# Delta-rule attention and two MoE layers: four-way state update, a longer look-ahead, and another engine pair for the masking of the query products

## The chip, the core and the metric

The kernel runs on one core of a Trainium2 chip. The core's engines are TensorE (PE in the profile; PEld is its weight load), VectorE (DVE), ScalarE (ACT), GpSimd (POOL) and SyncE (SP, which issues the transfers). The metric is the device time of one execution in microseconds.

## The reference

Attention by the delta rule over 4 batches, 8 heads, 768 positions, head size 48, with a state matrix for each batch and head; then two feed-forward layers over 3072 tokens.

```python
for t in range(S):
    y[:, :, t] = einsum('bhd,bhde->bhe', q[:, :, t], state)
    v_old = einsum('bhde,bhd->bhe', state, k_n[:, :, t])
    state = state + beta_t * einsum('bhd,bhe->bhde', k_n[:, :, t], v[:, :, t] - v_old)
x = y as (3072, 384)
h = x @ w1_in; x = (h * tanh(softplus(h))) @ w1_out      # 384 -> 2048 -> 384
h = x @ w2_in; out = (h * clip(h + 3, 0, 6) / 6) @ w2_out
```

Here `k_n` is `k` divided by its norm.

## The kernel before, in words

**Chunks.** The sequence is cut into 24 chunks `t` of 32 positions; the four batches lie side by side in the 128 partitions, 32 each, and heads in pairs `j`, halves `r`. For a chunk the keys and queries are transposed (`T_pe`, L419, copied to `kqt` by ScalarE, L425), and multiplied with the keys (`G_pe`, L439, two PSUM banks `gps`, one for each `r`). The key part times beta and a lower mask becomes `an` (`G_ew`, L457); the query part times an upper mask becomes `mt` (`G_ew2`, L463, VectorE). Two chunks of `an` go through DRAM to the layout of a forward substitution on VectorE (`substs`, tiles `ash`, `tp`, `tmp`, L716 and L723), which inverts them; the result comes back as `pt`, scaled by beta on GpSimd (`scale`, L744).

**Recurrence** (`rec`, L825). For each chunk, in this order: K (`state_pe`, `ksps`, keys times state), `r` (L862, the values less that), U (`U_pe`, `ups`, `pt` times `r`), the query round (`state_pe`, `yps`, queries times state), `u` copied to SBUF, MU (`MU_pe`, `mt` times `u` on top of the query round), the update round (`S_mm`, L808, `dsps`, keys times `u`), and eight VectorE additions to the state `sbd` (`S_add`, L820). The output is transposed (`X_pe`) and copied to `xst` (L972), four chunks to a block of 512 tokens.

The update round has two halves of two batches each, one PSUM bank a half; within a half the two batches alternate:

```python
for b in (2 * half, 2 * half + 1):
    p = slice(C * b, C * (b + 1))
    nc.tensor.matmul(out=S_part(b, r)[:, j, :], lhsT=kp(t)[p, j, r, 0:D], rhs=ut[t][p, 2 * j + r, :], ...)
```

`S_part(b, r)` lies in bank `b // 2`, partitions from `64 * (b % 2)`. A float32 matmul call shows in the trace as two matmul records and two weight loads.

**Look-ahead.** Inside chunk `t` (from 4 or 5 on) the recurrence also issues the transposes of chunk `t + 4`, after U, and the Gram products of chunk `t + 3`, after K. Keys have five buffers in rotation (`kp`), `kqt` and `mt` four; a key load waits for the update round that last read its buffer. The norms of the keys (`norms`: a square, a sum, a power on GpSimd, L399, and small VectorE steps, L401 to L367) and the beta mask (`beta_mask`, L407) must be done before the Gram products are issued. Chunks 0 to 7 are prepared by other functions (`prep_k`, `matrices`, `preps`, `preps_m`).

**MoE.** The first layer runs in six blocks of 512 tokens, 16 units each: nine `hps` matmuls (`mm1`, L1120), Mish on ScalarE (L1151), a split of the result into two parts (`ghi` on ScalarE, L1126, and `glo` on GpSimd, L1160), nine `o` matmuls (`mm2_t`, L1141). A block's input is split from `xst` into `xh` (ScalarE, L1098) and `xl` (VectorE, L1102). Weights are split in the same way by a lane of ScalarE and VectorE steps (`Weights`). The second layer follows, without the attention.

**Order.** `Flow` writes the program: each piece of work is a generator that names the events it needs, the engine and an estimated time, and the piece that can begin first (plus its penalty) is emitted next. Each engine then runs its queue strictly in that order. In the stage of the attention, five PSUM banks are shared by recurrence, look-ahead and `hps`; `room` grants a bank and `release` gives it back.

Of the kernel before, what the change touches and what calls it, by code (L numbers as in the profile page):

```python
# [16 lines left out]
C = 32  # L17
NKP = 5
NQP = 2
NVT = 3  # L20
NKQ = 4

RATE, TOKENS = 32.0, 110.0
# [103 lines left out]
def tile_delta_rule__moe_mish__moe_hardswish(  # L127
# [38 lines left out]
    with tc.manual_schedule():  # L166
# [84 lines left out]
        def load_heads(src, dst, t, engs=None):  # L251
# [5 lines left out]
            return flow.landed(2.2)  # L257

        def kp(t):
            return kpad[t % NKP]  # L260

# [33 lines left out]
        def loads_k():  # L295
            for t in range(NKP, NS):
                yield f"S{t - NKP}"
                yield LOAD
                flow.ev[f"kk{t}"] = load_heads(k, kp(t).rearrange("p j r d -> p (j r) d")[:, :, 0:D], t)
                if t >= 8:  # L300
                    flow.ev[f"k{t}"] = flow.ev[f"kk{t}"]
# [120 lines left out]
        def T_ew(t, i):  # L422
            if i == 0:
                kqt[t] = ap_.tile([128, NP, B, 2, C], F32, tag=f"kqt{t % NKQ}", name="kqt")
            nc.scalar.activation(  # L425
# [34 lines left out]
        def G_ew2(t, r):  # L460
            if r == 0:
                mt[t] = ap_.tile([128, H, C], F32, tag=f"mt{t % 4}", name="mt")
            nc.vector.tensor_tensor(  # L463
# [115 lines left out]
        def masks():  # L579
            for t in range(8, NS):  # L580
                yield f"n{t}"
                yield f"mt{t - 1}" if t > 8 else "G7"
                yield "POOL", 0.7
                beta_mask(t)
                flow.set(f"mb{t}")

        def G_post(t):

            for r in range(2):
                yield "DVE", 0.28  # L590
                G_ew(t, r)
            for r in range(2):
                yield "DVE", 0.28
                G_ew2(t, r)
                release(("G", t, r))
            flow.set(f"mt{t}")
            if t % 2:
# [3 lines left out]
                nc.sync.dma_start(out=an[g].rearrange("p s j -> s p j"), in_=x.rearrange("s t h j -> s (t h) j"))  # L601
                flow.ev[f"ad{g}"] = flow.landed(1.5)

        def T_post(t, i):
# [194 lines left out]

        def S_mm(t, half):  # L800

            if t == 0 or t >= 4:
                dps[half] = bank(("S", half), [128, 2, NP, D], "dsps")
            for r in range(2):
                for j in range(NP):
                    for b in (2 * half, 2 * half + 1):
                        p = slice(C * b, C * (b + 1))
# [4 lines left out]
                        )  # L812
            if half:
                flow.set(f"S{t}")

# [9 lines left out]
        def rec():  # L825


            for t in range(NS):
# [79 lines left out]
                if t < 4:  # L908
                    if t == 0:
                        yield room(("S", 0), ("S", 1))  # L910
                    yield "PE", 1.1, None, 64
                    for half in range(2):
                        S_mm(t, half)
                    flow.add(mu(t), pen=0.02)
# [4 lines left out]
                if not last:  # L919
                    yield room(("S", 0), ("S", 1))  # L920
                yield "PE", 1.0 if last else 2.6, None, 128
                MU_pe(t)
                flow.add(take_y(t), pen=0.05)
                if not last:
                    for half in range(2):
                        S_mm(t, half)
                    for b in range(B):
# [530 lines left out]
        flow.add(norms(), pen=0.05)  # L1458
        flow.add(preps(), pen=busy(0.1, 0.05), margin=busy(0.0, 1.0))
        flow.add(preps_m(), pen=busy(0.3, 0.05), margin=busy(0.0, 1.0))  # L1460
        flow.add(masks())
# [44 lines left out]
```

## Time and profile before

| | |
|---|---|
| median of 3 runs | 1072.04 us (1067.91 to 1072.45) |
| profiled execution | 1072.36 us |
| its span, first to last instruction | 1070.5 us |
| granted TensorE clock, mean | 0.988 |
| TensorE busy | 1039.6 us (97%) |
| VectorE, ScalarE, GpSimd busy | 647.8, 444.9, 213.1 us |

Busy TensorE time is modelled from starts, so a busy TensorE may still be waiting inside a matmul. The chain of the profile is followed back from the last instruction; it is on TensorE for 87% of the span.

### The profile page before, as it was taken

The numbers are of one execution on the slowest core, as the hardware profiler recorded it, in microseconds if no ns is written. First come the engines' busy times: TensorE is split into PE (matmuls) and PEld (weight loads), VectorE is DVE, ScalarE is ACT, GpSimd is POOL, SyncE is SP. The second block draws the span as 40 slices with busy tenths as digits, with TensorE's granted clock in tenths as the row PEclk, the third lists the DMA queues.
The fourth block names the chain that finished last, engine by engine and source line by source line (L and its number), as shares of the span: only waits on it lengthen the run. The fifth ranks groups of instructions, "written<-read, shape, count | busy, mean of one in ns | idle before, by whom it ended". The sixth has DMA issues, their size and how long they took to land.

```text
span 1070.5 us, 30628 instructions
## 1 busy us (share of the span) xinstructions
PE 1039.6 (97%) x13242; PEld 866.3 (81%) x13242; DVE 647.8 (61%) x1492; ACT 444.9 (42%) x884; POOL 213.1 (20%) x224
## 2 busy tenths in 40 slices
PE   8899998999999999999999999999999999999997
PEld 5566876777888788878887887999999999999996
DVE  6667977969496757849671799944333343333432
ACT  4346445433453344344432656534333343333432
POOL 3303333233333333332322332000000000000000
PEclk9899999989999999999999999999999999999999
DMA  5644244241423332241310543402001020010101
GB/s 94 148 125 100 68 123 112 61 86 32 83 41 80 58 67 67 46 77 31 70 21 15 185 134 120 140 1 60 1 14 46 1 59 1 14 46 1 30 1 30
DMA packets 149063, 66.64 MB, mean 62 GB/s; under 512 B 133024, under 2 KB 136096, under 8 KB 148928
## 3 DMA queue, kind: packets, MB, share of 16 engines
q1 hardware_dynamic: 146432, 63.84, 24.7%
q8 instruction: 104, 1.70, 0.6%
q10 hardware_dynamic: 2496, 0.84, 0.4%
q14 instruction: 31, 0.25, 0.1%
HBM read 51.02 MB, written 13.63 MB: 60 GB/s over the span
## 4 chain that ended last, share of the span: by engine, by line
PE 87%; DVE 7%; issue 2%; ACT 1%; POOL 1%; DMA 1%; POOLq 0%; ACTq 0%; DVEq 0%; SPq 0%
PE hps L1120 35%; PE p L1278 19%; PE o L1141 14%; PE warm L1437 3%; PE dsps L808 3%; PE tps L419 2%; PE gps L439 2%; PE yps L778 2%; PE ksps L758 2%; PE ups L768 2%; PE qps L665 2%; PE yps L758 1%; DVE cw L1065 1%; DVE cw L1062 1%; PE xps L956 1%
## 5 line engine op out<-in xcount | busy, mean ns | idle before, releaser
L1120 PE MATMUL hps<-xh,wih 128*128 128x512 f32 x576 | 229.3, 398 | 6.7 <-DVE mt L463 3.6
L1120 PE MATMUL hps<-xl,wih 128*128 128x512 f32 x576 | 227.3, 395 | 3.3 <-DVE xl L1102 3.3
L1120 PE MATMUL hps<-xh,wil 128*128 128x512 f32 x576 | 227.3, 395 | 0.0
L1160 POOL TENSOR_TENSOR glo<-g,ghi 128x512 fp32r<-128x512 f32 x96 | 130.4, 1358 | 307.4 <-ACT ghi L1126 244.7
L1253 DVE SCALAR_TENSOR_TENSOR r<-r,hps 128x512 f32<-128x512 f32 x96 | 66.1, 688 | 162.4 <-ACT r L1251 162.4
L1251 ACT ACTIVATE r<-hps,half_c 128x512 f32<-128x512 f32 x96 | 66.1, 689 | 171.3 <-PE hps L1120 171.2
L1151 ACT ACTIVATE g<-hps 128x512 f32<-128x512 f32 x96 | 57.1, 595 | 183.9 <-PE hps L1120 179.0
L1120 PEld LDWEIGHTS hps<-xh,wih 128*128 128x128 f32 x576 | 108.5, 188 | 29.3 <-issue 4.5
L1278 PE MATMUL p<-woh,glo 128*128 128x384 f32 x384 | 129.6, 337 | 0.0
L1278 PE MATMUL p<-woh,ghi 128*128 128x384 f32 x384 | 129.4, 337 | 0.0
L1278 PE MATMUL p<-wol,ghi 128*128 128x384 f32 x384 | 129.0, 336 | 0.0
L1120 PEld LDWEIGHTS hps<-xl,wih 128*128 128x128 f32 x576 | 108.5, 188 | 23.8 <-DVE xl L1102 4.7
L1120 PEld LDWEIGHTS hps<-xh,wil 128*128 128x128 f32 x576 | 108.6, 188 | 23.0
L716 DVE TENSOR_TENSOR tmp<-tp,ash 128x126 f32<-128x126 f32 (+22 forms) x248 | 99.1, 400 | 39.0 <-DMA ash<-ad 32.6
L1141 PE MATMUL o<-ghi,woh 128*128 128x512 f32 x288 | 114.2, 396 | 0.0
L1141 PE MATMUL o<-ghi,wol 128*128 128x512 f32 x288 | 113.9, 395 | 0.0
L1259 DVE TENSOR_TENSOR glo<-r,ghi 128x512 fp32r<-128x512 f32 x96 | 66.5, 693 | 57.0 <-ACT ghi L1126 56.5
L1126 ACT ACTIVATE ghi<-r 128x512 fp32r<-128x512 f32 x96 | 60.6, 631 | 64.6 <-DVE r L1253 64.5
L1141 PE MATMUL o<-glo,woh 128*128 128x512 f32 x288 | 84.2, 394 | 0.0
L723 DVE TENSOR_TENSOR tp<-tp,tmp 128x126 f32<-128x126 f32 (+22 forms) x248 | 79.5, 321 | 7.1
L820 DVE TENSOR_TENSOR sbd<-sbd,dsps 48x192 f32<-48x192 f32 x152 | 53.5, 352 | 43.6 <-PE dsps L808 40.6
L1278 PEld LDWEIGHTS p<-woh,ghi 128*128 128x128 f32 x384 | 72.3, 188 | 3.9
(139 smaller groups left out, 1436.3 us busy)
## 6 DMA issues: line engine op xcount, KB each, us to landing
raw<-in_moe_w_in_dram SPq DMA_DIRECT2D x24, 512.0 KB, 3.7
raw<-in_moe_w_out_dram SPq DMA_DIRECT2D x32, 384.0 KB, 3.1
vt<-in_v_dram SPq DMA_DIRECT2D x96, 48.0 KB, 2.2
x2d<-x2out SPq DMA_DIRECT2D x6, 768.0 KB, 4.0
x2in<-x2d SPq DMA_DIRECT2D x6, 768.0 KB, 6.2
kpad<-in_k_dram SPq DMA_DIRECT2D x88, 48.0 KB, 2.3
qpad<-in_q_dram SPq DMA_DIRECT2D x88, 48.0 KB, 2.1
out_dram<-osb SPq DMA_DIRECT2D x22, 192.0 KB, 3.1
```

What stands on the lines that cost most here:

```text
L716: nc.vector.tensor_tensor(out=tv, in0=x[:, 0:m, j:j + 1].to_broadcast([128, m, n]), in1=a[:, j + 1:C, j:j + 1].rearrange("p i o -> p o i") ...
L723: nc.vector.tensor_tensor(out=x[:, 0:m, j + 1:C], in0=x[:, 0:m, j + 1:C], in1=tv, op=ALU.add)
L820: nc.vector.tensor_tensor(out=o, in0=o, in1=S_part(b, r), op=ALU.add)
L1120: nc.tensor.matmul(out=ps[0], lhsT=w[:, kk, c], rhs=xhl[n][xi][:, kk, :], start=(kk == 0 and x == 0), stop=(kk == KD - 1 and x == 2))
L1126: nc.scalar.activation(out=hi, in_=g, func=ACTF.Copy)
L1141: nc.tensor.matmul(out=acc[i][dc], lhsT=w[:, e, 128 * dc:128 * (dc + 1)], rhs=a, start=(f == 0 and x == 0), stop=(f == KF - 1 and x == 2))
L1151: nc.scalar.activation(out=g, in_=ps, func=ACTF.Mish)
L1160: nc.gpsimd.tensor_tensor(out=lo, in0=g, in1=hi.bitcast(F32), op=ALU.subtract)
L1251: nc.scalar.activation(out=r, in_=ps, func=ACTF.Relu, scale=1.0 / 6.0, bias=half_c)
L1253: nc.vector.scalar_tensor_tensor(out=r, in0=r, scalar=1.0, in1=ps, op0=ALU.min, op1=ALU.mult)
L1259: nc.vector.tensor_tensor(out=lo, in0=r, in1=hi.bitcast(F32), op=ALU.subtract)
L1278: nc.tensor.matmul(out=acc[n][s], lhsT=a[:, c], rhs=w[:, e, :], start=(f == 0 and x == 0), stop=(f == KF - 1 and x == 2))
```

## The change

The update round takes all four batches in turn, in one group instead of two halves. From chunk 9 on, transposes are issued five chunks ahead, and from chunk 10 on, Gram products four chunks ahead; chunk 13 is prepared by a generator of its own (`extra`), in buffers that the weight conversion of the first layer has given up, so that keys have six buffers from there on, and `kqt` and `mt` five. For chunks 8 to 23 the query products are copied out of PSUM by ScalarE and masked by GpSimd in SBUF; the banks of the Gram products are released after these copies and the multiplies by beta. The next beta mask waits for the multiply by beta, no longer for `mt`.

```diff
+TX = 13
+        def slot(t, n):
+            while t > TX:
+                t -= n + 1
+            return "x" if t == TX else t % n
         def kp(t):
-            return kpad[t % NKP]
+            i = slot(t, NKP)
+            return more["k"] if i == "x" else kpad[i]
         def loads_k():
             for t in range(NKP, NS):
-                yield f"S{t - NKP}"
+                yield "more" if t == TX else f"S{t - NKP - (t > TX)}"
...
         def masks():
-                yield f"mt{t - 1}" if t > 8 else "G7"
+                yield f"an{t - 1}.1" if t > 8 else "G7"
...
         def G_post(t):
+            flow.add(M_post(t), pen=0.05)
             for r in range(2):
                 yield "DVE", 0.28
                 G_ew(t, r)
-            for r in range(2):
-                yield "DVE", 0.28
-                G_ew2(t, r)
-                release(("G", t, r))
-            flow.set(f"mt{t}")
+                flow.set(f"an{t}.{r}")
...
+        def extra():
+            yield "lo1.27"
+            more["k"], more["m"] = [x2p.tile([128, 512], F32, tag="x2", name=f"x{n}") for n in "km"]
...
+            nc.gpsimd.memset(more["k"][:, :, :, D:64], 0.0)
+            flow.set("more")
+            yield f"k{TX}"
+            yield f"q{TX}"
+            yield f"Tq{TX - 1}"
...
+            for i in range(2):
+                T_pe(TX, i)
+                flow.add(T_post(TX, i), pen=0.05)
+            flow.set(f"Tq{TX}")
+            yield f"kq{TX}"
+            yield f"mb{TX}"
...
+            G_pe(TX)
+            yield from G_post(TX)
+
+        def M_post(t):
+            m = slot(t, 4)
+            m = mt[t] = more["m"] if m == "x" else ap_.tile([128, H, C], F32, tag=f"mt{m}", name="mt")
+            for r in range(2):
+                yield "ACT", 0.3
+                G_raw(t, 1, r, m)
+                yield f"an{t}.{r}"
+                release(("G", t, r))
+            yield "POOL", 0.66
+            nc.gpsimd.tensor_tensor(out=m, in0=m, in1=masku.rearrange("p (o c) -> p o c", o=1).to_broadcast([128, H, C]),
+                                    op=ALU.mult)
+            flow.set(f"mt{t}")
...
-        def S_mm(t, half):
+        def S_mm(t):
             if t == 0 or t >= 4:
-                dps[half] = bank(("S", half), [128, 2, NP, D], "dsps")
+                for half in range(2):
+                    dps[half] = bank(("S", half), [128, 2, NP, D], "dsps")
             for r in range(2):
                 for j in range(NP):
-                    for b in (2 * half, 2 * half + 1):
+                    for b in range(B):
...
-                tk = t + 4 if 4 <= t < NS - 4 else None
+                tk = t + 4 if 4 <= t < TX - 4 else t + 5 if TX - 4 <= t < NS - 5 else None
-                tg = t + 3 if 5 <= t < NS - 3 else None
+                tg = t + 3 if 5 <= t < TX - 3 else t + 4 if TX - 3 <= t < NS - 4 else None
...
-                yield "PE", 1.0 if last else 2.6, None, 128
+                yield "PE", 1.0 if last else 2.0, None, 128
```

## Rows read from the trace of the kernel before

**Rows 1.** Busy time by stretch: start:end, length, then each engine's busy us.
```profile
100.00:214.00 114.00, 108.17 (x2309) 86.01 (x2307) 96.44 (x231) 55.83 (x125) 35.69 (x30) 0.99 0.35 89
214.00:661.00 447.00, 441.27 (x6356) 357.22 (x6356) 312.52 (x823) 192.16 (x411) 150.87 (x141) 0.99 0.31 70
```
**Rows 2.** Waits of TensorE: waiter, releaser: us in total, times, longest.
```profile
PE hps L1120 <- DVE mt L463: 3.6, 5, 1.2
...
PE hps L1120 <- DVE xl L1102: 3.3, 2, 2.6
PE hps L1120 <- DVE bnat L367: 2.6, 1, 2.6
```
**Rows 3.** Timeline of TensorE in chunk 11: start, us, line, tiles, records.
```profile
292.66 0.86 PE L439 MATMUL gps<-kqt 48*32 48x64 f32 x64
...
297.07 0.88 PE L768 MATMUL ups<-r,pt 32*32 32x48 f32 x64
297.89 0.87 PE L758 MATMUL yps<-sbd,kqt 128*32 128x96 f32 x32
...
300.41 0.88 PE L778 MATMUL yps<-u,mt 32*32 32x48 f32 x64
301.22 1.51 PE L808 MATMUL dsps<-u,kpad 32*48 32x48 f32 x64
```
**Rows 4.** The update round's line: records, ns min/median/max, first and last start.
```profile
L808 PE MATMUL dsps<-u,kpad x1472: 202/203/312, 47.7 to 571.7; 32*48 32x48 f32 x184
```
**Rows 5.** The chain of waits in chunk 2: start us, us, what.
```profile
78.51 0.84 PE dsps L808 x30
79.35 0.73 issue
...
81.01 1.19 PE warm L1437 x5
```
**Rows 6.** Timeline of ScalarE where blocks 1 and 2 begin.
```profile
212.63 0.49 ACT L972 ACTIVATE xst<-xps 128x384 f32<-128x384 f32 x1 [4.33 <-PE xps L956]
213.15 0.63 ACT L1098 ACTIVATE xh<-xst 128x512 fp32r<-128x512 f32 x1
...
308.34 0.49 ACT L972 ACTIVATE xst<-xps 128x384 f32<-128x384 f32 x1 [1.99 <-PE xps L956]
...
311.73 0.63 ACT L1098 ACTIVATE xh<-xst 128x512 fp32r<-128x512 f32 x1 [2.49 <-PE hps L1120]
```
**Rows 7.** Timelines of four engines, from chunk 13's Gram products to chunk 12's U.
```profile
275.05 0.86 PE L439 MATMUL gps<-kqt 48*32 48x64 f32 x64
...
291.83 0.43 DVE L716 TENSOR_TENSOR tmp<-tp,ash 128x31 f32<-128x31 f32 x1 [2.22 <-DMA ash<-ad]
...
309.21 0.56 DVE L862 TENSOR_TENSOR r<-vt,ksps 128x384 f32<-128x384 f32 x1
...
328.21 0.19 DVE L723 TENSOR_TENSOR tp<-tp,tmp 128x16 f32<-128x16 f32 x1
...
338.57 1.26 POOL L744 TENSOR_TENSOR pt<-pt,bnat 128x256 f32<-128x256 f32 x2
...
340.53 0.88 PE L768 MATMUL ups<-r,pt 32*32 32x48 f32 x64
```
**Rows 8.** Lines of the masking: records, ns min/median/max, first and last start.
```profile
L463 DVE TENSOR_TENSOR mt<-gps,masku x40: 242/284/295, 97.2 to 507.6; 128x128 f32<-128x128 f32 x40
...
L468 ACT ACTIVATE mt<-gps x8: 272/275/277, 20.2 to 35.0; 128x128 f32<-128x128 f32 x8
...
L478 POOL TENSOR_TENSOR mt<-mt,masku x4: 725/734/776, 20.7 to 35.4; 128x256 f32<-128x256 f32 x4
```
**Rows 9.** Timeline of all engines around 360 us.
```profile
358.26 1.28 POOL L1160 TENSOR_TENSOR glo<-g,ghi 128x512 fp32r<-128x512 f32 x1
358.33 1.24 DVE L401 TENSOR_SCALAR nn<-nn 128x8 f32<-128x8 f32 x1 [0.70 <-POOL nn L399]
...
361.10 0.47 PE L1120 MATMUL hps<-xh,wih 128*128 128x512 f32 x1 [0.92 <-DVE mt L463]
```

More of the change, by code (lines that the diff above doesn't have):

```diff
@@ L257, in load_heads @@
             return flow.landed(2.2)
+        more = {}
+        def slot(t, n):
+            while t > TX:
+                t -= n + 1
+            return "x" if t == TX else t % n
         def kp(t):
-            return kpad[t % NKP]
+            i = slot(t, NKP)
+            return more["k"] if i == "x" else kpad[i]
         def kp_first(t):
@@ L423, in T_ew @@
             if i == 0:
-                kqt[t] = ap_.tile([128, NP, B, 2, C], F32, tag=f"kqt{t % NKQ}", name="kqt")
+                n = slot(t, NKQ)
+                kqt[t] = (cvp.tile([128, NP, B, 2, C], F32, tag="r1", name="kqt") if n == "x" else
+                          ap_.tile([128, NP, B, 2, C], F32, tag=f"kqt{n}", name="kqt"))
             nc.scalar.activation(
@@ L461, in G_ew2 @@
             if r == 0:
-                mt[t] = ap_.tile([128, H, C], F32, tag=f"mt{t % 4}", name="mt")
+                n = slot(t, 4)
+                mt[t] = more["m"] if n == "x" else ap_.tile([128, H, C], F32, tag=f"mt{n}", name="mt")
             nc.vector.tensor_tensor(
@@ L602, in G_post @@
                 flow.ev[f"ad{g}"] = flow.landed(1.5)
+        def extra():
+            yield "lo1.27"
+            more["k"], more["m"] = [x2p.tile([128, 512], F32, tag="x2", name=f"x{n}") for n in "km"]
+            more["k"] = more["k"].rearrange("p (j r d) -> p j r d", j=NP, r=2)
+            more["m"] = more["m"][:, 0:H * C].rearrange("p (h c) -> p h c", h=H)
+            yield "POOL", 0.4
+            nc.gpsimd.memset(more["k"][:, :, :, D:64], 0.0)
[3 more added lines that the diff above has]
+            yield f"Tq{TX - 1}"
+            yield room(("T", TX, 0), ("T", TX, 1))
+            yield "PE", 0.8, None, 32
+            for i in range(2):
[4 more added lines that the diff above has]
+            yield f"mb{TX}"
+            yield room(("G", TX, 0), ("G", TX, 1))
+            yield "PE", 0.8, None, 64
+            G_pe(TX)
[12 more added lines that the diff above has]
+            flow.set(f"mt{t}")
         def T_post(t, i):
@@ L812, in S_mm @@
                         )
-            if half:
-                flow.set(f"S{t}")
+            flow.set(f"S{t}")
         def S_add(t, b):
@@ L910, in rec @@
                         yield room(("S", 0), ("S", 1))
-                    yield "PE", 1.1, None, 64
-                    for half in range(2):
-                        S_mm(t, half)
+                    yield "PE", 0.8, None, 64
+                    S_mm(t)
                     flow.add(mu(t), pen=0.02)
@@ L924, in rec @@
                 if not last:
-                    for half in range(2):
-                        S_mm(t, half)
+                    S_mm(t)
                     for b in range(B):
@@ L1459, in tile_delta_rule__moe_mish__moe_hardswish @@
         flow.add(preps(), pen=busy(0.1, 0.05), margin=busy(0.0, 1.0))
+        flow.add(extra(), pen=0.05)
         flow.add(preps_m(), pen=busy(0.3, 0.05), margin=busy(0.0, 1.0))
```

## The prediction

> **What bounds the kernel now.** I read the busy time by stretch first, to see which engine fills each stage. From 100 to 661 us, where the attention chunks run between the units of the first MoE layer, TensorE is busy in all but 12 us of 561 [rows 1]; VectorE, the next, is busy in 409 of them. So a TensorE microsecond taken out of this stage is worth up to a microsecond, as long as nothing else comes to set the pace. Second, the waits of TensorE: the largest inside this stage are of `hps` matmuls that found their PSUM bank still held by the masking of the query products (`mt`, 3.6 us in five waits, and one of 2.6 us put down to `bnat`, which stands beside `mt` on the same queue), and of the first `hps` of a block on its input `xl` (3.3 us in two) [rows 2]. Third, the timeline of TensorE in one chunk, for the price of each group of small matmuls: U, the query round, MU, the update round (`dsps`) and the Gram products G [rows 3]. The update round is the odd one: 1.51 us for 64 matmul records, where U and MU take 0.88 us for as many of the same 48 columns. It runs in 23 chunks (1472 records, 64 each) [rows 4].
>
> Fourth, whether the recurrence keeps up, because a block of MoE cannot start before its four chunks are written. In the timeline of ScalarE the last copy into `xst` begins at 212.63 and the split for block 1 at 213.15; for block 2 it is 308.34 and 311.73 [rows 6]. The reader is to see that the recurrence is only 0.5 to 3.4 us ahead: it is a second bound, just behind TensorE. What holds it is the inverse. Chunk 12 had its `r` at 309.21, and its U only at 340.53, because its `pt` was scaled at 338.57; that comes from a substitution that began at 291.83 and ended at 328.21, on a Gram matrix multiplied at 275.05 in chunk 10 [rows 7].
>
> **The change part by part.** *Update round.* Before, a half round alternates two row strips of the array (batches 0 and 1, then 2 and 3); after, all four are alternated. What decides is how many matmuls overlap. Two strips give 1.51 us for 64, 23.6 ns each. U and MU alternate four 32-row strips and take 0.88 us, 13.8 ns each [rows 3]. The query round, also four tiles but 96 columns, takes 0.87 us for 32, 27.2 ns each, twice U: with four tiles the time goes by the columns streamed [rows 3]. The new order has four row strips but only two column strips (batches 0 and 2 share one, in different banks). G tells whether that hurts: its two row halves share column strips, in different banks, with 64 columns. Four at a time would need 13.8 x 64/48 = 18.4 ns each, 1.18 us; it takes 0.86 us [rows 3]. So tiles on one column strip do overlap there. Bounds: nothing gained (1.51 stays) and U's 0.88. I take 0.88, the nearest in columns and strips: 0.63 us a round.
>
> The Trainium skill (TensorEngine Tiling, Restrictions and Gotchas, Gotcha 1) speaks against this: different row tiles write to different banks and cannot access one bank at the same time. The update uses two banks for four row tiles, so by that rule two would still run at a time and the round would stay at 1.51 us, the sum losing its largest term. U's four row tiles write the one bank of `ups`, at different partitions, at 13.8 ns, so the trace does not agree with the rule read that strictly; it is rival A below.
>
> How many rounds count: 19 of the 23 lie in the saturated stage (chunks 4 to 22), 19 x 0.63 = 12.0 us. For chunks 0 to 3 TensorE is filling time with `warm` matmuls right after the update [rows 5], so I take nothing of their 4 x 0.63 = 2.5 us and keep it as a bound. For chunks 4 to 7 I also take nothing: block 1 started 0.5 us after its last chunk was written [rows 6], and the look-ahead is not changed for them, so what TensorE saves there may be spent waiting for that chunk. That leaves 15 x 0.63 = 9.5 us.
>
> Cost of the denser order: MU and the update together become 128 matmuls in 1.76 us instead of 2.39. Among groups of small matmuls the chain of waits shows stretches of issue inside a group, one of 0.73 us [rows 5]. Between two such bursts here stand whole MoE units, so I take nothing; the bound is 0.73 in each of 15 chunks, 11 us.
>
> *Masking of the query products.* For chunks 8 to 23, two VectorE multiplies of 0.284 us go (16 x 0.57 = 9.1 us), and come back as two ScalarE copies of 0.275 us and one GpSimd multiply of 0.734 us [rows 8]: 8.8 us on ScalarE and 11.7 us on GpSimd. Neither is full: together ScalarE is busy 248 us and GpSimd 187 us of the 561 [rows 1]. These cover the cost; were GpSimd not free, each would delay the `glo` split behind it by 0.73 us. The gain is the bank: it now comes free after the two multiplies by beta and a ScalarE copy, no longer after two more instructions at the back of VectorE's queue. The wait at 360 us shows it: GpSimd's `glo` ran from 358.26, VectorE's tiny `nn` step took 1.24 us beside it, everything behind was late, and `hps` stood 0.92 us for `mt` [rows 9]. Bounds: none of the 3.6 us, and all of it plus the 2.6 [rows 2]. VectorE's queue can still hold the beta multiply up, so I take 2.5 us.
>
> The Trainium skill (SBUF — State Buffer, Who interferes with whom) says that a VectorE instruction with two SBUF inputs, or in a two-port mode, and a GpSimd instruction that reads SBUF shut each other out for a whole instruction. The `nn` step beside `glo` agrees. By that rule the 16 new multiplies could cost VectorE up to the 11.7 us they last; it would not move the sum, as VectorE is not what sets the end, but it is what rival C lives on.
>
> *Look-ahead.* Transposes and Gram products are the same instructions in another place; one chunk (13) gets them on its own, in buffers that weight conversion has left, and one small memset is added. On TensorE this costs nothing. K loads for later chunks are issued one chunk sooner relative to use, on SP, with the same count. The beta mask and the norm must be ready one chunk sooner, which is a new place to wait on VectorE and GpSimd. What it brings: the product for chunk 12's inverse moves up by about a chunk. The substitution needed 291.83 to 328.21, and U followed `pt` by 2 us [rows 7], so the recurrence of chunks 12 to 23 may come forward by up to one chunk, a quarter of the 95.7 us between the last `xst` copies of two blocks [rows 6], 24 us. It has no term of its own: it is what lets the 9.5 us through, because without it the lead of 0.5 to 3.4 us would be used up after two or three blocks of 2.5 us each.
>
> Sum: 9.5 + 2.5 = 12.0 us. The profiled execution took 1072.36 us (span 1070.5 and 1.9 around it), 0.03% from the median, so I make it 1060.4, and say 1060.
>
> **The rivals.** *A, the update round stays as it is* (banks or column strips), or its gain goes into issue stalls. For it: only two banks; stalls of this kind exist [rows 5]. Against: U and G [rows 3]. Only the bank waits are left: 1072.4 - 2.5 = 1070.
>
> *B, the recurrence sets the pace.* TensorE saves 2.5 us a block but waits for `xst`. For it: leads of 0.5 and 3.4 us [rows 6]. Against: the inverse moves up. With the lead used once (3.4) and the bank waits (2.5): 1072.4 - 5.9 = 1066.5.
>
> *C, slower.* Place: GpSimd's queue. The new multiply waits there for ScalarE's copy, and `glo`, the norm's power and the beta mask wait behind it; the norm holds VectorE's queue, that the Gram bank, and that the next `hps`. Price: 2.6 us, the one wait of this kind before [rows 2]. To end over 1077.7 it must eat the 12 us and 5.3 more, 17.3/2.6, so seven such waits in 16 chunks. Time: 1078 to 1082. Before there was one.
>
> **How the numbers follow.** The forecast case has 0.75, A 0.10, B 0.10, C 0.05. Its own range: down to 12.0 + 2.5 + 3.6 + 2.6 + 3.3 = 24 us saved (all rounds, all waits of [rows 2]), 1048, which needs everything at once; up to 9.5 us saved less a few stalls, 1066. The range for 8 in 10 is 1051 to 1067.5: it takes in B, and leaves A, C and the far low end. A measurement of this kernel can tell about 0.5% (5.4 us) from no change, so faster means under 1066.7: the forecast case and half of B, 0.80. Same: A, the other half of B, 0.15. Slower: 0.05.
>
> **What would show it.** The update round: 0.88 us for 64 records in the timeline, and its busy time between 100 and 661 falling by 12 us; 1.5 us is A, 1.5 us with pieces and issue between is the feed. Bank waits: the lines of `hps` waiting for `mt` go or turn to ScalarE's copy. Look-ahead: the lead of `xst` over the split grows past 3.4 us in blocks 3 to 5; if TensorE instead waits for `xl` at block starts, it is B. C shows as `hps` waits behind `nn` and `glo`. The prediction is wrong if the stage from 100 us to the second layer shortens by less than 6 us, or by more than 20.

## The result, and the profile after

The changed kernel takes 1078.32 us (median of 6 runs, 1074.92 to 1080.76), the kernel before 1069.97 (6 runs beside it, 1066.94 to 1072.45). The ratio is 1.0071, 95% interval 1.0053 to 1.009: 7 to 8 us slower, where 1060 was forecast and the range ended at 1067.5. The profiled execution took 1077.8 us, span 1076.1.

Three of the steps can be seen to do what they were costed to do. First the timeline of TensorE, an update round and the matmul behind it, and the update round's line (busy us, mean ns, then idle time ahead of it):

```profile
290.57 0.93 PE L857 MATMUL dsps<-u,kpad 32*48 32x48 f32 x64
291.43 0.50 PE L1166 MATMUL hps<-xh,wih 128*128 128x512 f32 x1
...
L857 PE MATMUL dsps<-u,kpad 32*48 32x48 f32 x1344 | 21.0, 206 | 4.8 <-issue 4.8
```

Its 64 records span 0.93 us, where they spanned 1.51 [rows 3]; from its start to the next matmul a round takes 0.86 us, where it took 1.44. So 0.58 us a round are gained. Second, the waits of TensorE:

```profile
PE ksps L806 <- DVE sbd L868: 10.1, 16, 2.3
PE dsps L857 <- issue: 4.8, 5, 1.2
PE hps L1166 <- DVE xl L1148: 4.6, 8, 2.2
```

The waits of `hps` for `mt` and `bnat` [rows 2] are gone. In their place stands one that was not there: K waits 10.1 us, in 16 pieces, for VectorE's additions to the state (before, K waited 1.0 us in all, none of it for them). Third, the masking's lines, as costed from [rows 8], and the recurrence's later lead: chunk 12's U, the last `xst` copy of block 4's input, and the split that waits for it (timelines):

```profile
L481 ACT ACTIVATE mt<-gps 128x128 f32<-128x128 f32 x34 | 8.6, 274 | 13.5 <-DVE an L469 8.8 <-PE gps L451 4.7
...
L648 POOL TENSOR_TENSOR mt<-mt,masku 128x256 f32<-128x256 f32 x13 | 10.1, 779 | 24.2 <-ACT mt L481 24.1
```
```profile
327.52 0.88 PE L816 MATMUL ups<-r,pt 32*32 32x48 f32 x64
...
490.70 0.49 ACT L1018 ACTIVATE xst<-xps 128x384 f32<-128x384 f32 x1 [0.79 <-PE xps L1002]
...
513.76 0.63 ACT L1144 ACTIVATE xh<-xst 128x512 fp32r<-128x512 f32 x1 [2.76 <-PE hps L1166]
```

Chunk 12's U came at 327.52 in place of 340.53 [rows 7], and block 4's input was ready 23 us ahead of its use.

But the stage as a whole lost. From TensorE's timelines, the us from the first `hps` of a block to that of the next (for block 5, to the first `p` matmul, the output product of the second layer):

| | block 0 | 1 | 2 | 3 | 4 | 5 |
|---|---|---|---|---|---|---|
| before | 114.3 | 101.4 | 96.1 | 96.8 | 85.4 | 74.9 |
| after | 111.1 | 104.6 | 97.0 | 106.7 | 81.2 | 75.2 |

Block 1 lost what block 0 had gained, and block 3 lost most. Of its 9.9 us some four are work that moved: it now holds five update rounds in place of four, and block 4 two in place of three. The rest is new: TensorE is idle in block 3 for 5.6 us (1.2 before) and at 1.2 GHz for 10.2 us (none before).

Block 1 first. The same ScalarE rows for block 2, and the busy time by stretch:

```profile
312.71 0.49 ACT L1018 ACTIVATE xst<-xps 128x384 f32<-128x384 f32 x1 [5.03 <-PE xps L1002]
313.23 0.63 ACT L1144 ACTIVATE xh<-xst 128x512 fp32r<-128x512 f32 x1
```
```profile
100.00:214.00 114.00, 108.63 (x2254) 85.60 (x2253) 94.14 (x226) 59.69 (x137) 38.96 (x35) 0.97 0.37 92
214.00:661.00 447.00, 433.34 (x6317) 345.29 (x6316) 330.10 (x808) 199.01 (x437) 156.93 (x152) 0.98 0.33 74
```

Block 2's input came 4.4 us later than before, and its split followed at once (0.5 us; 3.4 in [rows 6]). TensorE's busy time between 214 and 661 us fell by 7.9 us, and VectorE's rose by 17.6 [rows 1]. The chain that ended last was 87% TensorE before; now it leaves TensorE. The page's shares, then the shares of the chain from 225 to 316 us (most of block 1 of the changed kernel) and from 411 to 518 us (its block 3):

```profile
PE 54%; DVE 19%; DMA 2%; issue 2%; POOL 1%; SPq 1%; ACT 1%; DVEq 0%; POOLq 0%; ACTq 0%
```
```profile
by line: DVE tmp L764 26.1%; DVE tp L771 20.6%; DVE sbd L868 12.0%; DMA ash<-ad 9.7%; issue 5.5%; POOL nn L409 3.7%; PE ksps L806 2.6%; SPq L254 1.9%; PE o L1187 1.7%; SPq L751 1.6%; DVE an L469 1.5%; PE hps L1166 1.5%; PE xps L1002 1.4%; S
by line: DVE tmp L764 27.7%; DVE tp L771 24.6%; DVE sbd L868 12.9%; issue 5.1%; DMA ash<-ad 4.4%; POOL nn L409 3.1%; PE hps L1166 3.0%; DMA td<-tp 2.7%; DVE xl L1148 2.7%; SPq L776 1.7%; PE o L1187 1.5%; PE ksps L806 1.4%; DVE nn L411 1.3%;
```

In the kernel before, the window from 225 to 316 us of the chain read:

```profile
by line: PE hps L1120 35.2%; PE o L1141 32.0%; PE dsps L808 6.3%; PE yps L778 3.6%; PE ksps L758 3.5%; PE gps L439 3.5%; PE tps L419 3.4%; PE ups L768 2.7%; PE yps L758 2.6%; PE xps L956 2.1%; DVE nn L401 1.4%; POOL nn L399 0.8%; ACT ghi L1
```

Now the substitution (`tmp`, `tp`) and the state additions carry it. Here is the end of block 1: TensorE's timeline, then VectorE's.

```profile
303.51 0.84 PE L857 MATMUL dsps<-u,kpad 32*48 32x48 f32 x55
305.59 0.31 PE L857 MATMUL dsps<-u,kpad 32*48 32x48 f32 x9 [1.25 <-issue]
308.19 0.50 PE L806 MATMUL ksps<-sbd,kqt 128*32 128x96 f32 x2 [2.29 <-DVE sbd L868]
...
310.36 1.49 PE L806 MATMUL ksps<-sbd,kqt 128*32 128x96 f32 x26 [0.23 <-DVE sbd L868]
311.77 0.90 PE L1002 MATMUL xps<-ident,y 128*128 128x128 f32 x3
312.60 1.19 PE L451 MATMUL gps<-kqt 48*32 48x64 f32 x64
...
316.40 0.80 PE L1166 MATMUL hps<-xl,wih 128*128 128x512 f32 x1
```
```profile
307.14 0.28 DVE L764 TENSOR_TENSOR tmp<-tp,ash 128x70 f32<-128x70 f32 x1
307.33 2.97 DVE L868 TENSOR_TENSOR sbd<-sbd,dsps 48x192 f32<-48x192 f32 x8
```

No matmul of the MoE is left between 300.1 and 313.9 us. TensorE ends the update at 305.9; VectorE, busy with the substitution, begins the additions at 307.33, and they take 2.97 us; K follows piece by piece. From 308.1 to 318.3 the granted clock is 1.2 GHz: the Gram products take 1.19 us in place of 0.86 [rows 3], and an `hps` record 0.63 to 0.80 us where one at 2.4 GHz takes 0.39. Such stretches in the stage add up to 27.3 us, against 10.2 before.

The waits of K come in three such groups of about 3 us, in blocks 0, 1 and 3. The one in block 3 is of another kind: VectorE's and TensorE's timelines together.

```profile
463.86 0.93 PE L857 MATMUL dsps<-u,kpad 32*48 32x48 f32 x64
464.72 0.50 PE L1166 MATMUL hps<-xh,wih 128*128 128x512 f32 x1
...
468.30 0.84 PE L1187 MATMUL o<-glo,woh 128*128 128x512 f32 x3
470.04 0.38 DVE L764 TENSOR_TENSOR tmp<-tp,ash 128x128 f32<-128x128 f32 x1
470.33 2.96 DVE L868 TENSOR_TENSOR sbd<-sbd,dsps 48x192 f32<-48x192 f32 x8
471.18 0.33 PE L806 MATMUL ksps<-sbd,kqt 128*32 128x96 f32 x2 [2.04 <-DVE sbd L868]
...
473.35 1.49 PE L806 MATMUL ksps<-sbd,kqt 128*32 128x96 f32 x26 [0.23 <-DVE sbd L868]
```

Eighteen MoE matmuls stand between the update and K here, and the recurrence is far ahead: this is chunk 19, which completes block 4's input, and that input was then ready 23 us early. Still TensorE waits, because VectorE begins the additions 5.5 us after the update, behind steps of the substitution; and the granted clock is 1.2 GHz for 6.8 us from 471.9. At the head of block 3, too, the input was 7.1 us early, and `hps` waited 2.15 us for `xl`, which stood on VectorE behind the norm (VectorE had waited 5.9 us for GpSimd's power step, and GpSimd 5.8 us for a transfer) and behind a step that GpSimd's `glo` had slowed (last section).

All of the loss lies in the stage. From the first `hps` to the first `p` it took 568.9 us before and 575.8 after. I split it over TensorE's timeline, each group of matmuls running to the start of the next, so that a wait counts to the group it follows:

| us | before | after | |
|---|---|---|---|
| update rounds | 27.3 | 24.4 | 19 x 0.86 = 16.3, and 8.1 of waiting |
| transposes ahead | 19.7 | 13.7 | the bank waits of `hps` had stood behind them |
| query rounds and MU | 33.4 | 32.3 | |
| K | 15.9 | 26.1 | waits for additions, and the clock |
| `hps` | 215.2 | 220.0 | waits for `xl`, and the clock |
| all else | 257.4 | 259.3 | |

The bare rounds gave 11.0 us and the bank waits about 6. Query rounds and MU gave 1.1 more. Some 25 us of new waits and slower matmuls took it all back: 8.1 behind the update, 10.2 in K, 4.8 in `hps`, 1.9 elsewhere. 25.0 less 18.1 is the 6.9 us by which the stage grew.

### The profile page after: what moved, and what is told of

Read it like the earlier page. It is cut to its first block, busy times and chain, and to the rows that moved or that the text cites. A ratio compares the mean times of both kernels' runs of the same rounds, so it can differ in the third digit from the quotient of the medians.

```text
span 1076.1 us, 30630 instructions
## 1 busy us (share of the span) xinstructions
PE 1037.3 (96%) x13252; PEld 856.9 (80%) x13252; DVE 656.9 (61%) x1460; ACT 453.7 (42%) x916; POOL 223.6 (21%) x241
## 4 chain that ended last, share of the span: by engine, by line
PE 54%; DVE 19%; DMA 2%; issue 2%; POOL 1%; SPq 1%; ACT 1%; DVEq 0%; POOLq 0%; ACTq 0%
PE hps L1166 25%; PE p L1324 19%; PE o L1187 6%; DVE tmp L764 6%; DVE tp L771 5%; DVE sbd L868 3%; DMA ash<-ad 2%; POOL nn L409 1%; PE ksps L806 1%; DVE cw L1111 1%; DVE xl L1148 1%; DVE cw L1108 1%; DMA td<-tp 1%; DVE nn L411 1%; PE ups L816 1%
## 5 line engine op out<-in xcount | busy, mean ns | idle before, releaser
L764 DVE TENSOR_TENSOR tmp<-tp,ash 128x126 f32<-128x126 f32 (+22 forms) x248 | 102.6, 414 | 31.6 <-DMA ash<-ad 24.7
L771 DVE TENSOR_TENSOR tp<-tp,tmp 128x126 f32<-128x126 f32 (+22 forms) x248 | 89.1, 359 | 7.3
L1324 PEld LDWEIGHTS p<-wol,ghi 128*128 128x128 f32 x384 | 72.1, 188 | 3.9
```

The source lines that it names most:

```text
L764: nc.vector.tensor_tensor(out=tv, in0=x[:, 0:m, j:j + 1].to_broadcast([128, m, n]), in1=a[:, j + 1:C, j:j + 1].rearrange("p i o -> p o i") ...
L771: nc.vector.tensor_tensor(out=x[:, 0:m, j + 1:C], in0=x[:, 0:m, j + 1:C], in1=tv, op=ALU.add)
L1324: nc.tensor.matmul(out=acc[n][s], lhsT=a[:, c], rhs=w[:, e, :], start=(f == 0 and x == 0), stop=(f == KF - 1 and x == 2))
```

## The experiments

The theories were: **T**, TensorE sets the pace and the loss is some new TensorE cost; **R**, the recurrence (VectorE's inverse and additions) sets the pace of the first blocks, so TensorE time saved there is worth nothing and VectorE work added there is dear; **O**, the order that the planned costs bring about places K where it waits; **N**, any new order gains or loses some us by accident. Every ratio below is to the kernel before on the same chip, with its 95% interval.

**One part at a time.** `s_only` has the four-way round and its shorter planned costs; `m_only` the masking on ScalarE and GpSimd; `l_only` the longer look-ahead; `s_m` the first two.

Against the changed kernel, `s_only`, `m_only` and `s_m` have

```diff
-TX = 13
+TX = 99
...
-        flow.add(extra(), pen=0.05)
```

`s_only` and `l_only`

```diff
-            flow.add(M_post(t), pen=0.05)
...
+            for r in range(2):
+                yield "DVE", 0.28
+                G_ew2(t, r)
+                release(("G", t, r))
```

`m_only` and `l_only` (which also plan the round as before)

```diff
-                    for b in range(B):
+                    for b in (2 * half, 2 * half + 1):
```

> Only the four-way update round and its planned cost. Theory L (the moved look-ahead is what slows the whole change: its extra preparation of chunk 13 and the earlier norms load VectorE while it inverts for chunk 10): the 0.58 us a round come through in part, 1061 to 1066 us. Theory M (the masking on ScalarE and GpSimd slows it): the same. Theory O (a shorter round makes the order place K directly behind the additions, and TensorE stands there because VectorE is later than planned): 1070 us or more, with waits of K on the state additions of several us.

> Only the masking moved to ScalarE and GpSimd, with the release of the Gram banks after it. Theory L and theory O: the bank waits of 6 us go, 1064 to 1068 us. Theory M: slower than before, 1074 us or more, with VectorE's substitution lines longer in total than the 99 and 80 us of before.

> Only the longer look-ahead with chunk 13 prepared on its own. Theory L: slower than before by 5 us or more, 1075 to 1082 us, the last copy for block 2 into its block later than the 308 us of before. Theories M and O: no change or a little faster, 1065 to 1071 us.

> Four-way update round and moved masking, look-ahead as before. Theory L: both gains, 1056 to 1062 us. Theory M: 1070 us or more. Theory O: 1070 us or more, with waits of K on the state additions.

Measured: `s_only` 1.0029 (1.0011 to 1.0047), `m_only` 1.0036 (1.0017 to 1.0054), `l_only` 1.007 (1.0045 to 1.0095), `s_m` 0.9977 (0.9957 to 0.9998). Each part alone is slower than before, and the look-ahead alone costs as much as the whole change. Two together are not the sum of two: the masking costs 0.36% on the kernel before and gives 0.52% on `s_only`, and `s_m`, at 1068 us, lies between the ranges that the theories gave it. In `l_only` the last copy into `xst` ahead of block 2, in ScalarE's timeline, came 8.2 us later than in [rows 6], and the split at once behind it:

```profile
316.52 0.49 ACT L1024 ACTIVATE xst<-xps 128x384 f32<-128x384 f32 x1 [5.62 <-PE xps L1008]
317.04 0.63 ACT L1150 ACTIVATE xh<-xst 128x512 fp32r<-128x512 f32 x1
```

Its blocks 1 and 2 took 106.8 and 104.5 us (101.4 and 96.1 before), and blocks 3 to 5 together 250.3 (257.1). So the look-ahead moves work out of late blocks, where little waited, into early ones, and loses 13.8 us there to gain 6.8 (block 2 holds five update rounds here in place of four). K's waits for additions have no part in this: they are 0.4 us in all of `l_only`.

**Room for the recurrence, and less work for TensorE.** `cut` leaves out every second step of the forward substitution; `s_cut` does so with the four-way round; `less_mm` leaves out the third product of `mm1` in blocks 0 to 3, 192 `hps` matmuls that follow each other every 0.227 us, some 43.5 us of TensorE work, and plans their units that much shorter.

```diff
-                for j in range(C - 1):
+                for j in range(0, C - 1, 2):
```
```diff
-                yield "PE", 3 * MM, 0
+                ws = ((wh, 0), (wh, 1), (wl, 0))[:2 if n < 4 else 3]
+                yield "PE", len(ws) * MM, 0
...
-                for x, (w, xi) in enumerate(((wh, 0), (wh, 1), (wl, 0))):
+                for x, (w, xi) in enumerate(ws):
```

> The kernel before with every second step of the forward substitution left out (the inverse is not computed), so that about 89 us of VectorE work go and TensorE's work stays. Theory R (the recurrence, paced by the inverse on VectorE, sets the time together with TensorE): the stage becomes TensorE's alone and the waits shrink, 1055 to 1064 us. If TensorE alone sets the pace already: 1068 to 1072 us.

> The four-way update round on top of the cut substitution. Theory R: now the whole saving of 19 rounds by 0.58 us comes out, 10 to 13 us below the cut kernel without it. Theory O (the order places K too early behind a shorter round): waits of K on the state additions stay at 6 us or more and the gain is under 6 us.

> The kernel before with the third product (low part of the first weights) left out of the first layer in its first four blocks: 192 groups of matmuls of 0.227 us, 43.5 us of TensorE work less, attention untouched. Theory R: the blocks wait for the recurrence, the time falls by less than 20 us. If TensorE sets the pace alone: by 40 us or more.

Measured: `cut` 0.9935 (0.9915 to 0.9955), `s_cut` 0.9835 (0.9804 to 0.9865), `less_mm` 1.0002 (0.9978 to 1.0025). Without 43.5 us of TensorE's work the kernel is as slow as with it; its waits of TensorE and its busy time by stretch show where the work went:

```profile
PE ksps L809 <- DVE sbd L874: 13.9, 21, 3.2
...
PE hps L1173 <- DVE xl L1154: 4.0, 5, 0.9
```
```profile
100.00:214.00 114.00, 104.26 (x2297) 81.87 (x2296) 98.22 (x240) 57.12 (x129) 33.29 (x30) 0.93 0.36 90
214.00:661.00 447.00, 424.01 (x6203) 337.53 (x6203) 306.45 (x824) 191.02 (x410) 149.93 (x140) 0.95 0.32 70
```

TensorE is idle for 33 us, and runs at 1.2 GHz for 61 us of the stage, which shows as busy time. So T alone falls: the stage was 98% busy on TensorE, and work taken off TensorE alone did not shorten it. R alone does not stand either. In `cut` the inputs of blocks 2 to 5 came 26 to 35 us ahead of their splits, and only 0.65%, 7 us, came of it: with the recurrence out of the way TensorE was nearly as long. By these two runs the two bounds lay within some 7 us of each other. With the substitution halved the four-way round with its planned costs gives 1.0%, 10.7 us, about all of its 11; but with the old planned costs it gives 4.7 us with this room and 8.0 without (`cut` to `s_oldcost_cut`, before to `s_oldcost`, below), where R would have it give more with room. (`cut` and `less_mm` also change the order, which alone is worth up to 20 us, below; 43.5 us is more.) The update round is itself a link of the recurrence, so that its gain does not tell the two bounds apart.

**The planned cost of the round.** The change also told the planner a shorter time for it. `s_oldcost` is `s_only` with the old figures, `plan_only` is the kernel before with the new ones, `s_latecost` is `s_only` with still longer ones, `sm_oldcost` and `sml_oldcost` are `s_m` and the changed kernel with the old ones. Within a pair the instructions are the same, but for some ten `warm` fillers ahead of the stage; what differs is where they stand.

For the three with the old figures (and 1.1 in place of 0.8 for chunks 0 to 3):

```diff
-                yield "PE", 1.0 if last else 2.0, None, 128
+                yield "PE", 1.0 if last else 2.6, None, 128
```

`plan_only` has the same edit the other way round; `s_latecost` has 3.2 and 1.4.

> The four-way update round alone, but planned with the old costs of 2.6 and 1.1 us. Theory O: the waits of K on the state additions vanish and the gain comes out, 1058 to 1064 us. Theory R: the waits of K vanish too, but the recurrence gets no faster, 1068 to 1074 us.

> The kernel before with one edit: its two-half update round stays, but is planned with the shorter costs of the changed kernel (2.0 in place of 2.6 in a chunk, 0.8 in place of 1.1 in the early ones). Every instruction is the same; only the order in which they are emitted differs. Theory O (the shorter planned cost places the next K products right behind the state additions, and TensorE stands there): slower than before by about what the four-way round lost to it, 12 us between the two versions of that round, so 1076 to 1086, with the waits of ksps on sbd up from 0.4 us to 5 us or more. Theory N (the order has no direction to it, any new order costs or gains some us by accident): 1064 to 1076 with those waits under 3 us. Theory O is taken, at 1078.

> The four-way round alone, planned longer than either kernel did: 3.2 in place of 2.0 (1.4 in place of 0.8 in the early chunks). Theory O (a longer planned cost puts other work of TensorE between the additions and the next K, which is what helps): as good as with 2.6, 1059 to 1066, ksps waiting on sbd under 2 us. Theory N (2.6 is only the value that the rest of the order was fitted to, and any other value loses): 1067 to 1076. I take 1064.

> The four-way round and the masking on ScalarE and GpSimd, without the longer look-ahead, planned with the old costs of the round (2.6 and 1.1). Theory O and the masking as a help (with the new costs the masking took 6.3 us off the four-way round: 1074.3 to 1068.0): 1056 to 1061, with ksps waiting on sbd under 3 us. Theory R (the recurrence sets the pace, and the masking slows VectorE's substitution through the shared port, as alone, where it cost 3.9 us): 1063 to 1068, not better than the four-way round with old costs alone (1062.5). I take 1060.

> The changed kernel in full, with one edit: the update round is planned with the old costs (2.6 and 1.1). Theory O (the planned cost is what turned the change into a loss): the 12 us between the two orders of the four-way round come back, 1063 to 1069, and the waits of ksps on sbd fall from 10.1 us to under 4. Theory L (the longer look-ahead is the loss: it loads VectorE while block 1 is waiting for the recurrence, and alone cost 7 us): 1072 to 1078. Half of each would be 1069 to 1072. I take 1068.

Measured: `s_oldcost` 0.9925 (0.9901 to 0.9949), `plan_only` 1.0072 (1.0046 to 1.0097), `s_latecost` 1.0116 (1.0082 to 1.0149), `sm_oldcost` 1.0005 (0.9983 to 1.0026), `sml_oldcost` 1.0068 (1.0045 to 1.009). The first two are for O: the new figures alone cost the kernel before 0.72%, and the old ones make the four-way round 0.75% faster than before, the fastest of the kernels that leave nothing out. The timeline of TensorE at chunk 11's update round, in `s_oldcost`:

```profile
301.28 1.06 PE L860 MATMUL dsps<-u,kpad 32*48 32x48 f32 x64
302.28 0.50 PE L1169 MATMUL hps<-xh,wih 128*128 128x512 f32 x1
...
306.58 0.87 PE L809 MATMUL ksps<-sbd,kqt 128*32 128x96 f32 x32
```

and in `s_only`:

```profile
299.53 0.93 PE L860 MATMUL dsps<-u,kpad 32*48 32x48 f32 x64
301.87 0.33 PE L809 MATMUL ksps<-sbd,kqt 128*32 128x96 f32 x2 [1.41 <-DVE sbd L871]
...
304.03 1.49 PE L809 MATMUL ksps<-sbd,kqt 128*32 128x96 f32 x26 [0.29 <-DVE sbd L871]
```

With the longer figure eighteen MoE matmuls stand between the update and K, and cover VectorE's additions; with the shorter one they have been spent earlier, K waits, and its clock falls. But as a rule O falls: a still longer figure gave the slowest kernel of all, 1.9% over the one with 2.6 and outside every range expected, the masking with the old figures came out 12 us over the 1060 expected, and the changed kernel did not get faster by them. What is left is N, with O as one of its mechanisms.

**The look-ahead.** `sm_cut` and `sml_cut` are `s_m` and the changed kernel with the halved substitution; `sml_late17` begins the look-ahead a block later; `s_l` is `s_only` with the look-ahead; `s_oldcost_cut` is `s_oldcost` with the halved substitution.

The edit of `sml_late17` is the one below; those of the others have been shown.

```diff
-TX = 13
+TX = 17
```

> The four-way round and the masking, without the longer look-ahead, with every second step of the forward substitution left out, so that the recurrence has room. Theory R (the masking costs VectorE time, which is dear only where the recurrence sets the pace; its gain is the bank waits of TensorE, 2.5 to 6 us): 2 to 6 us under the four-way round with the same cut (1052.9), 1047 to 1051. Rival (the masking costs or gains by accident of order): 1052 to 1060. I take 1049.

> The changed kernel in full, with every second step of the forward substitution left out, so that the recurrence has room. Theory R (the look-ahead loses because its VectorE work falls in the blocks that wait for the recurrence): it costs nothing here, within 3 us of the same kernel without the look-ahead. Theory P (the look-ahead costs TensorE by itself, through waits for banks and buffers and a worse mixture at the ends of blocks): 6 to 10 us above that kernel. I take R, at 1049.

> The changed kernel with the longer look-ahead begun a block later: chunk 17 in place of 13 is the one that is prepared on its own, transposes are five chunks ahead from chunk 13 and Gram products four ahead from chunk 14. Theory R (the loss arises in block 1, whose recurrence the added VectorE work delays): block 2 starts as without the look-ahead (309 us, not 314), the lost time is at most that of one more such boundary, 1068 to 1073. Theory P: 1075 to 1080, as with 13. I take 1071.

> The four-way round with its new costs and the longer look-ahead, without the masking. Against the four-way round alone (1074.3) this is a fourth pair for the look-ahead. Theory R or P (it loses in whatever order): 1079 to 1085. Theory N (chance of the order): 1066 to 1078. I take 1081.

> The four-way round planned with the old costs (2.6 and 1.1), with every second step of the forward substitution left out, so that the recurrence has room. With the new costs this kernel took 1052.9. Theory R (which order the planned cost gives matters only where the recurrence has no room): within 3 us of it, 1050 to 1056, in place of the 12 us between the two orders without the cut. Rival (the order costs TensorE by itself): 5 us or more away, most likely below, 1042 to 1048. I take 1052.

Measured: `sm_cut` 0.9817 (0.9791 to 0.9844), `sml_cut` 0.9852 (0.9825 to 0.9879), `sml_late17` 1.0035 (1.0018 to 1.0052), `s_l` 1.0046 (1.0027 to 1.0064; its median, 1073.5, stands beside 1067.3 for before on its chip), `s_oldcost_cut` 0.9891 (0.9869 to 0.9912). `s_l` fell to N. Begun a block later, the look-ahead costs 0.58% over `s_m` in place of 0.94%: block 2 starts 211.6 us after block 0, as in `s_m` (211.2) and not as in the changed kernel (215.7; the kernel before has 215.8). With room for the recurrence it costs 0.35%, between what R and the rival expected, and the two intervals overlap. `s_oldcost_cut` was a miss: with room, the old figures lose 0.56%, so the order matters there too, with the other sign.

**The clock.** `after_fill` puts 28 small matmuls, which nobody reads, ahead of chunk 12's K in the changed kernel.

```diff
+                    if t == 12:
+                        for _ in range(28):
+                            z = ident.bitcast(BF16)
+                            nc.tensor.matmul(out=kps.rearrange("p j d -> p (j d)")[:, 0:256], lhsT=z[:, 0:128], rhs=z, start=True, stop=True)
                     state_pe(t, 0, kps)
```

> The changed kernel with 28 small matmuls, whose results nobody reads, ahead of the K product of chunk 12, where TensorE has no MoE work left and waits for the state additions; order and planned costs of all else are kept. Theory C (much of the loss is the clock: from 308 to 318 us TensorE is granted 1.2 GHz, K, the transposes, the Gram products and the first nine hps of block 2 take 10.4 us where 5 are enough): the half-clock stretch there shrinks or goes, 3 to 5 us come back, 1073 to 1075. Theory W (the clock is low where TensorE waits anyway, for the recurrence, so it costs little): 1077 to 1080. I take 1075.

Measured: 1.0038 (1.0014 to 1.0062), 0.33% or 3.5 us under the changed kernel, known to 0.3%. The timeline of TensorE:

```profile
304.43 3.23 PE L901 MATMUL ksps<-ident 128*128 128x256 bf16 x28
307.59 0.36 PE L806 MATMUL ksps<-sbd,kqt 128*32 128x96 f32 x4
...
309.03 0.85 PE L806 MATMUL ksps<-sbd,kqt 128*32 128x96 f32 x26 [0.41 <-DVE sbd L868]
...
310.28 0.86 PE L451 MATMUL gps<-kqt 48*32 48x64 f32 x64
311.59 0.51 PE L1170 MATMUL hps<-xh,wih 128*128 128x512 f32 x1 [0.45 <-ACT xh L1148]
312.80 0.63 PE L1170 MATMUL hps<-xl,wih 128*128 128x512 f32 x1 [0.70 <-DVE xl L1152]
```

K's last 26 records take 0.85 us in place of 1.49, the Gram products 0.86 in place of 1.19; then TensorE waits at the head of the block, and the clock falls after all, from 313.0 to 316.4. From the start of the update round to block 2's first `o` it takes 13.9 us in place of 15.0. So the profiles show 1.1 us at this place, and the time lies between the two ranges expected. The profiled execution is 4.5 us shorter as a whole, but 1.4 of that lie ahead of the stage and 2.2 in block 3, where nothing was edited; that this clock is worth 3 to 4 us is not shown.

**All pairs.** Differences of the ratios above, in percent of the kernel before (0.1% is 1.07 us). Each ratio is known to some 0.2 to 0.3%, so a difference to 0.3 or 0.4%, and smaller ones tell nothing:

| part | pairs | differences |
|---|---|---|
| four-way round, same planned costs | before to `s_oldcost`; `plan_only` to `s_only`; `cut` to `s_oldcost_cut` | -0.75, -0.43, -0.44 |
| shorter planned costs | before to `plan_only`; `s_oldcost` to `s_only`; `sm_oldcost` to `s_m`; `sml_oldcost` to after; `s_oldcost_cut` to `s_cut` | +0.72, +1.04, -0.28, +0.03, -0.56 |
| masking | before to `m_only`; `s_only` to `s_m`; `s_oldcost` to `sm_oldcost`; `s_l` to after; `sm_cut` over `s_cut` | +0.36, -0.52, +0.80, +0.25, -0.18 |
| look-ahead | before to `l_only`; `s_only` to `s_l`; `s_m` to after; `sm_oldcost` to `sml_oldcost`; `sm_cut` to `sml_cut` | +0.70, +0.17, +0.94, +0.63, +0.35 |

The round gains in all three, 4.6 to 8 us; the look-ahead gains in none, 2 to 10 us lost, of which three pairs are clear of the uncertainty; the other two have no sign of their own.

## Why the prediction was wrong

**The step that failed** is the pricing of the look-ahead at nothing ("On TensorE this costs nothing", "It has no term of its own"), and beside it the order: the round's shorter planned costs stood in the diff and were not priced at all. From before to after by way of `s_oldcost`, `s_only` and `s_m`, the round gave 8.0 us (9.5 taken), its planned costs took 11.1, the masking gave 5.6 (2.5 taken) and the look-ahead took 10.1. By way of `plan_only`, `s_only` and `s_l`, the planned costs took 7.7, the round gave 4.6, the look-ahead took 1.8 and the masking 2.7. Each figure is known to 3 or 4 us, and they depend on the order in which the parts are added; both ways, what was put at nothing took more than the priced parts gave.

**The condition behind the sum** failed with it: "a TensorE microsecond taken out of this stage is worth up to a microsecond, as long as nothing else comes to set the pace". What came to set it, in places, was VectorE: K waits 10.1 us for its additions, and the clock falls behind these waits. The second bound was seen, 0.5 to 3.4 us behind [rows 6], and rival B was made of it, but not that it was this close: `less_mm` took 43.5 us out and got 0.0% back. Where the order was kept (`s_oldcost`), on the other hand, most of the round's saving did come through, in blocks 1 to 4 alike (1.6, 2.2, 1.6 and 0.9 us).

**The look-ahead** was to be "what lets the 9.5 us through", at no cost on TensorE. The leads came: 7.1, 23.1 and 34.1 us for the inputs of blocks 3, 4 and 5 (3.1, 0.5 and 3.3 before). They let nothing through in block 3, the longest of them against before. To get there its transposes, Gram products and masks were done in block 1, where chunks 8 to 11 were themselves late: in the changed kernel chunk 10's U came at 286.4 us (281.5 before, 280.4 in `s_m`), chunk 11's at 300.1 (297.1 before). The step costed what is issued and not when; measured, it lost 6 us in the mean of five pairs (0.56%).

**The planned cost**, as a difference of order alone, moved the kernel before by +7.7 us.

**The update round** was right: 0.93 us for 0.88 forecast, 0.58 us saved for 0.63. The trace does not agree with the Trainium skill's rule on banks (TensorEngine Tiling (Array Packing), Restrictions and Gotchas, Gotcha 1), read as allowing two tiles at a time here: the four row tiles share two banks and still run nearly at the pace of U (0.93 and 0.88 us for 64 records). Rival A falls. In the time of the kernel the round is worth 4.6 to 8 us of the 9.5 taken. The bound for issue inside the denser groups, 11 us, came out at 4.8 (five pieces in front of `dsps`), of which 2.5 lie in the stage.

**The bank waits** went, all 6.2 us rather than 2.5, and the masking's two prices were right to 0.05 us a piece. Its cover was not: VectorE was no longer to be had for nothing. In `m_only` the substitution's two lines are (busy us, mean ns)

```profile
L764 DVE TENSOR_TENSOR tmp<-tp,ash 128x126 f32<-128x126 f32 (+22 forms) x248 | 104.6, 422 | 49.2 <-POOL tp L757 22.6 <-DMA ash<-ad 19.5
L771 DVE TENSOR_TENSOR tp<-tp,tmp 128x126 f32<-128x126 f32 (+22 forms) x248 | 83.6, 337 | 7.3
```

against 99.1 and 79.5 us before: 9.6 us more for the same 496 instructions. In all five pairs with and without the masking they are longer, by 4.2 to 12.6 us. The Trainium skill (SBUF — State Buffer, Who interferes with whom) was cited for up to 11.7 us from the new multiplies; the trace agrees in kind, but in `m_only` only 3.5 of the 9.6 us stand beside them (16 steps, against steps of the same shape with no GpSimd instruction beside them). The rest stands beside older GpSimd work, `glo` and `pt` above all, which fell on more of the substitution. The prediction waved it through because VectorE "is not what sets the end". On the chain of blocks 1 and 3 it is.

**The rivals.** B had the mechanism, with a gain of 5.9 us where a loss came: it let the recurrence keep its pace, and did not ask what the change adds to it, nor what TensorE's clock does when TensorE waits. C had the sign and the size (1078 to 1082), but by luck: the waits for a bank that it was made of went, and the one large `hps` wait left with GpSimd's queue ahead of it is the 2.15 us at block 3's head.

**Open.** Which order is good is not explained by one rule: the pairs with the same instructions differ by -6 to +20 us. K's waits do not tell it: `sml_late17` has more of them than the changed kernel (11.2 us) and is faster, `l_only` has almost none and is as slow. No run shows what block 3 would take if VectorE did the additions ahead of the substitution steps. And what the look-ahead costs where the recurrence has room (0.35%) is hardly more than the measurement can tell.

## What to carry to other kernels

An engine that is busy 98% of a stage is the only bound only if the work that feeds it is well ahead; look at how long each input had been ready when it was used, and where that is under a microsecond, price every edit by what it adds to the late chain too, not only by what it takes off the busy engine. A lead is not enough by itself: in block 3 the inputs were 7 to 23 us early, and TensorE still stood, because its queue held a step whose input came last on another engine's queue. In a program whose order comes from estimated times, an estimate is an edit: keep the old figures for a first run and change them by themselves, since a new order alone was worth up to 2% here. Work moved ahead is not free where the earlier place is the tight one; begin it after the stretch whose inputs are late (a block later, it cost 0.58% here in place of 0.94%).

## What was not expected of the hardware

Waiting costs twice: where TensorE had stood waiting (2.29 us and more ahead of K at 308 us), it was granted 1.2 GHz for 3.4 to 10.2 us on end, into the next block's full-size matmuls (0.63 us a record for 0.39). Such stretches added up to 13.7 us in the stage with the fill, for 27.3 without, in one execution each, and the time is counted as busy time, which hides it in the busy share.

The substitution ran slower beside GpSimd. Two of its steps of the same shape in the changed kernel, one beside a `glo` and one with GpSimd at rest:

```profile
410.45 1.28 POOL L1206 TENSOR_TENSOR glo<-g,ghi 128x512 fp32r<-128x512 f32 x1
410.58 1.22 DVE L764 TENSOR_TENSOR tmp<-tp,ash 128x30 f32<-128x30 f32 x1
...
280.86 0.21 DVE L764 TENSOR_TENSOR tmp<-tp,ash 128x30 f32<-128x30 f32 x1
```

In the kernel before, the 60 steps that run mostly beside a `glo` are together 30 us longer than steps of the same shapes with no GpSimd instruction beside them (29 us in `l_only`, 38 in the changed kernel). That is a sixth of the substitution's 179 us, and none of it was in the prediction's account of what holds the recurrence.
